# The second stage of an inverse transform, recorded with the last token group last, and a new issue order

## The chip, the cores and the metric

One Trainium2 chip, of which the kernel uses one core. The metric is the device time of one execution in microseconds. Matrix products run on TensorE (PE in the profile; its weight loads are PEld), element-wise work on VectorE (DVE) and ScalarE (ACT); transfers are issued mostly from SyncE's queue (SP) and are carried out by 16 DMA engines.

## The reference

The input `A_u` is 2048 tokens by 512 channels, all float32. It is normalised over the channels (xn). One branch is a state-space convolution along the tokens: a kernel K of 2048 taps per channel is built from 128 complex exponentials, and xn is convolved with it through transforms of twice the length. The other branch is a spatial-shift MLP. The output is gated and added to the input:

```
x = A_u
xn = layernorm(x)
K = einsum("dn,dnl,dn->dl", C, exp(dt*A*l), dt*B).real
s = irfft(rfft(pad(xn)) * rfft(pad(K)))[:L] + xn * Dskip
h = gelu(layernorm(xn) @ w1)                    # 512 -> 512
hs = concat(h shifted by +1, -1, +2, -2 tokens per channel quarter) @ w2
x1 = xn + hs
b = x1 + gelu(layernorm(x1) @ w3) @ w4          # 512 -> 1376 -> 512
out = x + s * silu(b)
```

## The kernel before

The tokens lie in the tile `X` as 128 partitions by 16 positions `s` by 512 channels. Two positions make a *group*; there are eight, and `GROUPS` is 1, 2, 3, 4, 5, 6, 7, 0, the order in which the MLP takes them. The convolution works on two halves of 256 channels, called a (`hf` 0) and b (`hf` 1) here.

The work is recorded in this order: loads; `params` (phases and magnitudes of the exponentials); `token_mixing` (first normalisation, w1, the shift and w2, the first transform stage of xn, preparation of w3 and w4 as pairs of float16); `tables(0)`, which builds K for half a in eight chunks (waves on ACT, products on DVE, sums on PE, stored to DRAM); the MLP of two groups; `kstage1(0)` and `products(0)` (transform of K, product of the spectra, first inverse stage for half a, result stored to `scr_Zda`); `tables(1)`; the MLP of the other six groups; `kstage1(1)` and `products(1)` (the same for half b, result to `scr_Zdb`); `gate` (a silu per group over the finished MLP result in `X`); `inverse` for both halves and all groups; `finish` per group (adds the input `xr`, stores to the output in four pieces of 128 KB).

`inverse(hf, g)` loads 0.5 MB of the intermediate result (`zin`), runs 16 small matrix products with `is2` into a pair of PSUM banks, and multiplies that half of the group's channels of `X` by the result. It takes its pair from `pp_pair`, which alternates between `duo[2]` and `duo[3]` (pc and pd in the profile, both 128 x 2 x 512). `products(1)` calls `pp_pair` 16 times ahead of it, so the first `inverse` gets pd. A later product into a pair has to wait until the multiplication that reads the earlier one is done. The multiplication of a group in turn has to follow the group's silu, and the silu the group's last down-projection (`mlp`, accumulated in `duo[0]`, pa in the profile; the up-projections go to pb).

Recording doesn't set the order in which things are issued. Every recorded operation (some are groups made with `plan.together`) goes through `Plan.add`, which finds what it depends on from the places that it reads and writes, in the recorded order. `Plan.order` then simulates the four queues (PE, ACT, DVE, SP) with estimated costs: at each step it takes the queue that is free first and, among its operations that are ready, the one with the smallest due time. The due times are the table `DUE`, one number per recorded operation. Constants correct them: `SWITCH` is added where ACT would have to load another function table, `KEEP` where PE would change the part of its array that it uses, `PREFERP`, `AVOIDP`, `PREFER`, `AVOID` where an operation may run on ACT or on DVE. So the result is a fixed list for each queue, which the engine works off in order. `ISSUE` is the estimated time that a transfer takes on its issuing queue, `TURNED` the estimated time of a transposing transfer on the DMA engines; the transposing transfers turn the normalised MLP input (`x1s`) into `x1T`.

## Time and profile before

| | us |
|---|---|
| median of 3 runs (lowest, highest) | 564.03 (563.72, 564.52) |
| the profiled execution | 563.24 |
| span of the profiled execution, first to last instruction | 561.4 |

The profile is of one execution; its span leaves out what lies before the first and after the last instruction. The mean granted TensorE clock of this execution was 0.991. All instructions that went through the planner carry line L532, where it issues them, so they are told apart by their tiles: x1T, w3h, ghl, w4h, pa and pb belong to the MLP, pt, mag and pab to the tables, kin, uin, pr to the products of spectra, zin to `inverse`, xr to `finish`. L529 is the loading of a function table on ACT. The DMA transfers over the whole span:

| | MB |
|---|---|
| read from HBM | 64.46 |
| written to HBM | 37.75 |

### The profile page before, as it was taken

Reading aid. Unit: us, or ns where it says so; the run is one execution under the profiler, and the core shown is the slowest. Engines: PE = TensorE matmul, PEld = TensorE weight load, DVE = VectorE, ACT = ScalarE, POOL = GpSimd, SP = SyncE. Lnnn points to the kernel's source line nnn. Section 1 sums busy time; section 2 is a strip of 40 time slices with the busy share of each in tenths; the row PEclk is TensorE's granted clock in tenths of the full one; section 3 lists DMA queues with packets and bytes.
Section 4 is the critical chain, followed back from the end, with each engine's and each line's share of the span. In section 5 each row is a group of like instructions: output and inputs, shape, how many; then the busy total and the mean of one; then the engine's idle time right before and its main releaser. Section 6 shows DMA issues by size and latency. Waiting matters only on the chain.

```text
span 561.4 us, 14315 instructions
## 1 busy us (share of the span) xinstructions
PE 530.3 (94%) x6098; PEld 348.1 (62%) x6098; DVE 452.7 (81%) x748; ACT 395.1 (70%) x573; POOL 0.7 (0%) x6
## 2 busy tenths in 40 slices
PE   9879999999999979999999999999999999999982
PEld 9866776767435438556577567557656567566530
DVE  5799996599999999999999999998344357753466
ACT  3789997699983989998899997976326424232520
POOL 0000000000000000000000000000000000000000
PEclk9999999999999999999999999999999999999996
DMA  8952767762666442576532745346898959949987
GB/s 212 234 163 66 242 219 257 238 201 76 214 209 218 147 97 79 103 225 226 144 105 62 176 141 133 86 161 190 242 291 288 303 173 284 263 165 255 280 261 219
DMA packets 86593, 107.35 MB, mean 191 GB/s; under 512 B 31680, under 2 KB 65728, under 8 KB 85632
## 3 DMA queue, kind: packets, MB, share of 16 engines
q1 hardware_dynamic: 85760, 104.33, 63.0%
q10 hardware_dynamic: 768, 2.10, 1.2%
q8 instruction: 48, 0.79, 0.6%
q14 instruction: 17, 0.14, 0.1%
HBM read 64.46 MB, written 37.75 MB: 182 GB/s over the span
## 4 chain that ended last, share of the span: by engine, by line
PE 65%; DVE 14%; DMA 8%; ACT 8%; issue 1%; SPq 1%; DVEq 0%; ACTq 0%
PE pb L532 26%; PE pa L532 21%; PE pc L532 10%; PE pd L532 8%; DVE pt L532 6%; DMA X<-in_A_u_dram 4%; DVE X L532 3%; ACT pt L532 3%; ACT mag L532 2%; DVE stats L532 2%; DMA wst<-in_B_w_dram 1%; DMA x1T<-x1s 1%; SPq L532 1%; ACT L529 1%; DMA scr_Kfa<-k1e 1%
## 5 line engine op out<-in xcount | busy, mean ns | idle before, releaser
L532 PE MATMUL pb<-x1T,w3h 128*128 128x256 f16 (+1 forms) x1056 | 123.0, 273 | 0.9 <-DMA x1T<-x1s 0.9
L532 PE MATMUL pa<-w4h,ghl 128*128 128x512 f16 (+1 forms) x528 | 120.9, 379 | 0.0
L532 PEld LDWEIGHTS <-w3h 128*128 128x128 f16 (+1 forms) x1056 | 102.4, 100 | 25.6 <-issue 11.3
L532 PEld LDWEIGHTS <-ghl 128*128 128x128 f16 (+1 forms) x528 | 49.6, 98 | 62.2 <-issue 7.1
L529 ACT ACT_TABLE_LOAD x54 | 69.3, 1283 | 5.2 <-DMA out_dram<-X 3.6
L532 ACT ACTIVATE pt<-pt 128x2048 f32<-128x2048 int32 x32 | 60.8, 1904 | 1.9 <-DVE pt L532 1.7
L532 PE MATMUL pb<-xT,w 128*128 128x256 f32 x256 | 59.6, 383 | 1.1 <-ACT xT L532 1.1
L532 DVE SCALAR_TENSOR_TENSOR ghl<-g,wsc,ghl 128x512 f16<-128x512 f32 (+1 forms) x48 | 33.5, 699 | 32.4 <-ACT ghl L532 32.3
L532 DVE TENSOR_TENSOR pt<-mag,pt 128x1024 f32<-128x1024 f32 x48 | 57.5, 1214 | 0.1
L532 PE MATMUL pd<-w,hT 128*128 128x512 f32 x116 | 52.9, 599 | 3.2 <-DVE X L532 2.3
L532 PEld LDWEIGHTS pb<-xT,w 128*128 128x128 f32 x256 | 47.1, 190 | 13.1 <-issue 3.2
L532 ACT ACTIVATE g<-pb,wsc 128x512 f32<-128x512 f32 (+1 forms) x48 | 30.9, 650 | 33.6 <-PE pb L532 31.2
L532 ACT ACTIVATE mag<-par 128x128 f32<-128x128 f32 x160 | 41.2, 454 | 4.6 <-DMA X<-in_A_u_dram 3.8
L532 ACT ACTIVATE ghl<-g,wsc 128x512 f16<-128x512 f32 (+1 forms) x33 | 22.4, 681 | 24.5 <-PE pa L532 23.5
L532 PEld LDWEIGHTS pd<-w,hT 128*128 128x128 f32 x116 | 21.4, 190 | 29.0 <-issue 23.9
L532 DVE TENSOR_TENSOR pt<-pt 128x2048 f32<-128x2048 f32 x16 | 36.5, 2282 | 2.0 <-ACT pt L532 2.0
L532 PEld LDWEIGHTS pc<-pt 128*32 128x32 f32 x2048 | 29.8, 110 | 10.5 <-issue 6.7
L532 PE MATMUL pc<-pt 128*32 128x64 f32 x2048 | 34.0, 220 | 2.1 <-DVE pt L532 1.8
L532 ACT ACTIVATE pt<-pt,halfpi 128x2048 f32<-128x2048 f32 x16 | 31.9, 1999 | 0.1
L532 DVE TENSOR_TENSOR pr<-pd,uin 128x1024 f32<-128x1024 f32 x16 | 19.1, 1217 | 11.7 <-PE pd L532 11.7
L532 DVE TENSOR_TENSOR pt<-pab 128x1024 int32<-128x1024 f32 x16 | 19.4, 1215 | 10.1 <-PE pc L532 10.1
L532 DVE TENSOR_TENSOR pr<-pd,kh 128x1024 f32<-128x1024 f32 x16 | 19.2, 1217 | 2.9 <-PE pd L532 2.9
(155 smaller groups left out, 753.8 us busy)
## 6 DMA issues: line engine op xcount, KB each, us to landing
wst<-in_B_w_dram SPq DMA_DIRECT2D x20, 512.0 KB, 3.8
scr_Ud<-ue SPq DMA_DIRECT2D x16, 512.0 KB, 4.0
uin<-scr_Ud SPq DMA_DIRECT2D x32, 256.0 KB, 4.5
cst<-c_gp SPq DMA_DIRECT2D x16, 384.0 KB, 4.6
scr_Uh<-uh SPq DMA_DIRECT2D x8, 512.0 KB, 5.2
scr_Kfa<-k1e SPq DMA_DIRECT2D x8, 512.0 KB, 2.8
kin<-scr_Kfa SPq DMA_DIRECT2D x16, 256.0 KB, 3.5
scr_Zda<-z1e SPq DMA_DIRECT2D x8, 512.0 KB, 5.6
```

Source lines behind the costliest of these rows:

```text
L529: self.engines["ACT"].preload_act_table_set(SETS[table])
L532: ins = [getattr(self.engines[op.eng], name)(*args, **kw).ins for name, args, kw in op.calls]
```

## The change

Three things change. In the recording, `inverse` runs over both halves for the first seven of `GROUPS`, and only then over both halves for the last one, group 0. For group 0 both halves write into one pair, always `duo[2]`, half a into the first 256 columns of each bank and half b into the other 256, and one multiplication over all 512 channels follows the second half; the first half returns without one. The number of matrix products is the same, there is one DVE operation less (1751 recorded operations, not 1752).

In the planner's estimates a transposing transfer takes 1.25 on its issuing queue, not 0.45, and 1.55, not 1.4, on the DMA engines.

And the whole table of due times is another, with another set of the constants that go with it. The diff without the table:

```diff
-TURNED = 1.4
+TURNED, TURN_ISSUE = 1.55, 1.25
 ISSUE = 0.45
-SHIFT, KEEP = 0.09, -134.72
+SHIFT, KEEP = 0.09, -41.4
...
-SWITCH = 57.29
-PREFERP, AVOIDP = 156.76, -96.02
-PREFER, AVOID = 81.81, -92.31
+SWITCH = 196.28
+PREFERP, AVOIDP = 150.95, -129.56
+PREFER, AVOID = -68.73, 92.63
...
-                cost = ISSUE
-                dma = TURNED if name == "dma_start_transpose" else dma_cost(aps)
+                cost, dma = (TURN_ISSUE, TURNED) if name == "dma_start_transpose" else (ISSUE, dma_cost(aps))
...
-        py = pp_pair()[:, :, :DH]
+        pair = duo[2] if g == GROUPS[-1] else pp_pair()
+        py = pair[:, :, ch if g == GROUPS[-1] else slice(0, DH)]
         with plan.together(cost=0.46):
             for r in range(4):
                 for a in range(2):
                     h = slice(64 * a, 64 * a + 64)
                     T.matmul(py[32 * r : 32 * r + 32, a], is2[h], zin[h, ORDER[r]], start=True, stop=True)
+        if g == GROUPS[-1]:
+            if hf == 0:
+                return
+            ch, py = slice(0, D), pair
         Xh = X[:, 2 * g : 2 * g + 2, ch]
         V.tensor_mul(Xh, Xh, py)
...
-    for hf in range(2):
-        for g in GROUPS:
-            inverse(hf, g)
+    for some in (GROUPS[:-1], GROUPS[-1:]):
+        for hf in range(2):
+            for g in some:
+                inverse(hf, g)
```

The due times run from -3272 to 2643 before and from -7486 to 7590 after. Those of the spectrum products (`spectrum` and the first inverse stage on PE) of half b in recorded order, and of group 0's MLP on PE:

| | before | after |
|---|---|---|
| spectrum products of half b | 819 to 1258 | 5268 to 6378 |
| the last three units of them | 837 to 1197 | 5272 to 6378 |
| up- and down-projections of group 0 | 984 to 1882 | 4670 to 7590 |
| products of `inverse`, groups 1 to 7, half a | 663 to 2390 | 6277 to 7404 |
| products of `inverse`, groups 1 to 7, half b | 420 to 1576 | 5508 to 7421 |
| products of `inverse`, group 0, half a and b | 525 and 1326 | 6467 and 4686 |

294 rows, old and new, of the table DUE are left out of this document.

## The prediction

> **What bounds the kernel now.** I read the page first (engine shares and the span in slices), then the busy time by stages, then the timeline and the chain of waits at the end, then the transfers there. The page says which engine is nearly full:
>
> ```profile
> span 561.4 us, 14315 instructions
> PE 530.3 (94%) x6098; PEld 348.1 (62%) x6098; DVE 452.7 (81%) x748; ACT 395.1 (70%) x573; POOL 0.7 (0%) x6
> ```
>
> A share of 94% is a mean over stages, so I cut the span where its character changes (busy us of each engine per stage):
>
> ```profile
> 41.00:120.00 79.00, 77.89 (x637) 57.58 (x637) 67.17 (x145) 69.69 (x88) 0.00 (x0) 1.00 0.59 197
> 120.00:220.00 100.00, 92.23 (x1230) 51.92 (x1229) 99.81 (x153) 87.52 (x150) 0.00 (x0) 1.00 0.49 158
> 220.00:500.00 280.00, 278.21 (x3445) 180.13 (x3443) 222.68 (x322) 195.12 (x248) 0.00 (x0) 1.00 0.65 190
> 500.00:542.50 42.50, 42.50 (x397) 24.05 (x397) 19.07 (x26) 15.35 (x19) 0.00 (x0) 1.00 0.93 254
> 542.50:561.40 18.90, 5.52 (x129) 1.61 (x128) 13.31 (x15) 1.06 (x1) 0.00 (x0) 0.74 0.64 188
> ```
>
> The columns are length, then PE, PEld, DVE, ACT, POOL, the granted clock, the share of the DMA engines, GB/s. From 120 to 220 DVE is full (99.81 of 100) and PE waits for it (100 - 92.23 = 7.77 us idle). From 220 to 542.5 PE is full: 278.21 of 280, then 42.50 of 42.50. In the last 18.90 us PE has 5.52 us of work and DVE 13.31. So 18.9 us of the span are a tail in which the engine that bounds the rest is mostly free. The timeline shows what it is made of:
>
> ```profile
> 537.18 5.36 PE L532 MATMUL pa<-w4h,ghl 128*128 128x512 f16 x24
> ...
> 542.57 1.28 DVE L532 SCALAR_TENSOR_TENSOR X<-pa,wsc,X 128x1024 f32<-128x1024 f32 x1 [2.60 <-PE pa L532]
> ...
> 543.89 1.06 ACT L532 ACTIVATE X<-X 128x1024 f32<-128x1024 f32 x1 [1.78 <-DVE X L532]
> ...
> 545.10 0.67 PE L532 MATMUL pc<-zin,is 64*32 64x256 f32 x16
> ...
> 546.70 0.68 DVE L532 TENSOR_TENSOR X<-X,pc 128x512 f32<-128x512 f32 x1
> ...
> 547.43 0.67 PE L532 MATMUL pc<-zin,is 64*32 64x256 f32 x16 [1.66 <-DVE X L532]
> ...
> 549.16 0.67 PE L532 MATMUL pc<-zin,is 64*32 64x256 f32 x16 [1.06 <-DVE X L532]
> ...
> 551.02 0.75 PE L532 MATMUL pc<-zin,is 64*32 64x256 f32 x16 [1.19 <-DVE X L532]
> ...
> 552.88 1.11 PE L532 MATMUL pc<-zin,is 64*32 64x256 f32 x16 [1.10 <-DVE X L532]
> ...
> 554.81 1.23 DVE L532 TENSOR_TENSOR X<-X,xr 128x1024 f32<-128x1024 f32 x1
> ```
>
> The last down-projection of the MLP (group 0) ends at 537.18 + 5.36 = 542.54. Its result goes through DVE (1.28) and the silu of group 0 on ACT (1.06, ending 544.95). After that come products of `inverse`, each followed by a multiplication and an addition on DVE, one after the other, to 554.81 + 1.23 = 556.04; the rest to 561.4, 5.36 us, is the last output stores.
>
> Why are so many inverse products left for the end? `inverse` takes its PSUM pair from `pp_pair`, which alternates: recorded in the order a1 to a7, a0, b1 to b7, b0 (a, b the channel halves), pc serves a2, a4, a6, a0, b2, b4, b6, b0 in that order. The multiplication that empties pc after a0 needs the silu of group 0, which needs the end of the MLP. So b2, b4, b6 cannot start before about 545 however early their data are there; they are the products at 547.43, 549.16 and 551.02, each waiting for a DVE X. The recorded order alone holds them back.
>
> **The change, part by part.**
>
> *The recorded order.* Group 0 goes last in both halves. The pc pair now serves a2, a4, a6, b1, b3, b5, b7 and then group 0; pd serves the others. No product of groups 1 to 7 is behind group 0's silu any more. Eight products fall after 542.4 in the timeline (starts 542.46, 542.92, 544.50, 545.10 and the four above); six of them are of groups 1 to 7 and may now run beside the last MLP group. Their price there is PE time, since PE is full:
>
> ```profile
> 536.65 0.59 PE pd L532 x16
> 537.25 5.30 PE pa L532 x24
> ```
>
> In the chain a product put between down-projections took 0.59 us. Six cost 6 x 0.59 = 3.5 us; if both products of group 0 are put ahead too, 8 x 0.59 = 4.7. I take the middle, 4.1: the MLP ends at 542.55 + 4.1 = 546.65.
>
> *The work of DVE that goes with them.* Of the 13.31 us in the last stage only the accumulation (1.28), two multiplications (2 x 0.68) and one addition (1.23) belong to group 0; 13.31 - 1.28 - 1.36 - 1.23 = 9.4 us move ahead of the MLP's end. From 500 to 542.5 DVE was busy for 19.07 of 42.50 us, so there are 23.4 us of room: cost nothing. If that room were not there when it is needed (the data late), the 9.4 us would stay on the path; that is the second rival.
>
> *One product for group 0.* Two multiplications of 128x512 (0.68 each) become one of 128x1024. The nearest row of that size, with one operand in PSUM:
>
> ```profile
> L532 DVE TENSOR_TENSOR pr<-pd,uin 128x1024 f32<-128x1024 f32 x16 | 19.1, 1217 | 11.7 <-PE pd L532 11.7
> ```
>
> So 1.22 instead of 1.36, 0.14 us less on the path. PE does the same 2 x 16 matmuls; only their place in PSUM differs.
>
> *The new tail.* After the MLP's end: accumulation and the step to ACT, 543.89 - 542.55 = 1.34; silu 1.06; multiplication 1.22 with a gap of 0.05; addition 1.23 with 0.02; together 4.92. Then the stores, 5.36 as now. Sum 546.65 + 4.92 + 5.36 = 556.9, against 561.4: 4.5 us less. The profiled execution took 563.24 us with a span of 561.4 (1.84 around it), the median of the runs shown is 564.03. On its own time: 563.24 - 4.5 = 558.7. The 5.36 is an upper value: stores of eight groups are crowded there now, and later only group 0's four are left at the end:
>
> ```profile
> L532 SPq DMA_DIRECT2D out_dram<-X x16: 314/315/1632, 537.9 to 556.7; - x16
> L532 ACTq DMA_DIRECT2D out_dram<-X x16: 321/382/1577, 537.9 to 556.9; - x16
> ...
> DMA to landing us min/median/max: 1.9/3.4/5.2
> ```
>
> With two issues of 0.38 on one queue and the shortest landing, 1.9, it would be 2.7; that lowers the sum by at most 2.7. I keep 5.36, the row of this place.
>
> *Is there room on the DMA engines?* All groups' stores but the last must get out before the end. The transfers from 535 on (busy share in 40 slices of 0.66 us, GB/s):
>
> ```profile
> DMA  9999999999832490008985989898839887997000
> GB/s 349 348 348 348 348 349 352 371 408 349 317 143 93 112 279 6 0 0 199 199 304 168 217 174 304 267 323 298 304 81 292 317 286 273 217 323 267 19 0 0
> ```
>
> The first ten slices are loads of `zin`, at about 349 GB/s until some 541; then there is a hole, and then the stores. 32 stores of 128 KB are 4.19 MB, of which four (0.52) went before 542. The other 3.67 MB at 290 GB/s, a middle value of the store slices, take 12.7 us: from 541.1 to 553.8, ahead of the 556.9. At 217, a low slice, 16.9 us and with 1.9 of landing 559.9. So the DMA engines stand just behind the new path; this gives the upper end of the case, 559.9 + 1.84 = 561.7.
>
> *The planner's constants.* `TURNED` and `TURN_ISSUE` only change what the planner assumes of a transposing transfer, from 0.45 us on SP to 1.25. The trace has
>
> ```profile
> L532 SPq DMA_TRANSPOSE x1T<-x1s x16: 1238/1276/5401, 203.8 to 485.7; - x16
> ```
>
> a median of 1.276, so the plan was wrong by 0.8 us at 16 places and is right now. No instruction gets dearer or cheaper. What it hid was small; the page puts down 0.9 us of PE's idle time in the whole span to an x1T:
>
> ```profile
> L532 PE MATMUL pb<-x1T,w3h 128*128 128x256 f16 (+1 forms) x1056 | 123.0, 273 | 0.9 <-DMA x1T<-x1s 0.9
> ```
>
> *The new order everywhere else.* Every due time is replaced (and `SWITCH`, `KEEP`, the preferences), so all four queues may differ from the first load on. The same instructions are issued, so the PE total stays. What can change is PE's idle time between 41 and 500: 1.11 + 7.77 + 1.79 = 10.7 us from the table of stages. Nothing in the trace says where the new order stands; I cost it at nothing and bound it by half of that idle time either way, 5.3 us, since the other half would need DVE to have gaps to close, and from 120 to 220 it has 0.19 us.
>
> *A rule against the change.* PE's clock falls in the tail: 0.74 granted in the last stage, and the product at 552.88 took 1.11 where others took 0.67. The Trainium skill, "TensorE: Matmul & The Clock Gate", Part 1, says that the array runs at half its clock after a window of about 3.4 us without enough activity. The trace agrees. If group 0's products were left until PE had rested, they would cost 1.11 - 0.67 = 0.44 us more each, and the sum would be 559.1 with one of them on the path. PE is busy right up to the silu here, so I do not add it.
>
> **The rivals.**
>
> 1. *More than the tail.* The new order also closes half of PE's idle time between 41 and 500: 558.7 - 5.3 = 553.4. For it: 7.77 us of idle lie in one stage. Against: DVE is full there, so only another choice of its work, not more of it, could help.
>
> 2. *The change does not do what it says.* The PSUM pair is free, but the data of half b come late. Its loads:
>
> ```profile
> L532 SPq DMA_DIRECT2D zin<-scr_Zdb x8: 382/1386/3235, 522.3 to 533.5; - x8
> ...
> DMA to landing us min/median/max: 5.1/9.9/12.2
> ```
>
> The last is issued at 533.5 and lands near 541, as the full DMA slices show. If the second half's spectrum is not finished earlier against the MLP than now, and the products wait, the 9.4 us of DVE stay behind the MLP, and only 0.14 goes: 563.1. Against: between 541 and the new end of the MLP, 546.65, there are 5 us even then, and the due times of the last spectrum products stand to those of group 0's MLP much as before (the last three units 5272 to 6378 beside 4670 to 7590 now, 837 to 1197 beside 984 to 1882 then), so nothing in the diff puts the data later.
>
> 3. *The order in the stage that DVE bounds gets worse* (slower). From 120 to 220 PE lives on what DVE hands it, and after 220 PE is full, so idle time gained there is never made up. The unit by which an order can go wrong is a table chunk:
>
> ```profile
> L532 DVE TENSOR_TENSOR pt<-mag,pt 128x1024 f32<-128x1024 f32 x48 | 57.5, 1214 | 0.1
> ...
> L532 DVE TENSOR_TENSOR pt<-pt 128x2048 f32<-128x2048 f32 x16 | 36.5, 2282 | 2.0 <-ACT pt L532 2.0
> ...
> L532 DVE TENSOR_TENSOR pt<-pab 128x1024 int32<-128x1024 f32 x16 | 19.4, 1215 | 10.1 <-PE pc L532 10.1
> ```
>
> (57.5 + 36.5 + 19.4) / 16 = 7.1 us of DVE per chunk. One chunk done ahead of what PE needs gives 558.7 + 7.1 = 565.8. It decides against the change when PE's idle time between 41 and 500 passes 10.7 + 4.5 = 15.2 us.
>
> 4. *The products stand in front of the MLP and wait* (slower). PE takes its queue in order:
>
> ```profile
> 492.95 1.47 PE L532 MATMUL pb<-x1T,w3h 128*128 128x256 f16 x12 [0.87 <-DMA x1T<-x1s]
> ...
> 494.35 2.00 PE L532 MATMUL pc<-pr,cst 64*128 64x256 f32 x16
> ```
>
> Where it waited 0.87 us for an x1T ahead of 492.95, the product behind it started only after that. Eight `zin` tiles of 0.52 MB at 349 GB/s need 12.0 us; if all eight products were queued ahead of the last down-projections, PE would go at the pace of the loads and idle for 12.0 - 8 x 0.59 = 7.3 us: 558.7 + 7.3 = 566.0. The Trainium skill, the same page, Part 3 ("The mechanism"), says that matmuls start and end in program order; by that rule a product that waits for its load holds back every down-projection behind it. The trace agrees at 492.95. Against the rival: with two PSUM pairs at most two products can be ahead of their multiplications, so a queue of eight cannot form unless it is put there on purpose.
>
> **How the numbers follow.** Forecast 558.7, chance 0.50, its own range 556.0 (shorter stores) to 561.7 (DMA bound). Rival 1, 553.4: 0.17. Rival 2, 563.1: 0.15. Rival 3, 565.8: 0.11. Rival 4, 566.0: 0.07. The range reaches from 553.2, just under rival 1, to 564.5, over rival 2 and up to a part of a chunk; what lies outside is rivals 3 and 4 and a little of 1, 2 in 10. A measurement of this kernel can tell about 0.2% (1.1 us) from no change, so faster means under 562.9 and slower over 565.2: 0.67 (forecast and rival 1), 0.15 (rival 2), 0.18 (rivals 3 and 4).
>
> **What would show it.** Right: in the new timeline, from the end of the last pa matmul to the end of the span some 10.3 us instead of 18.9; at most two products after it; one multiplication 128x1024 of X by pc; the MLP's end at 546 to 547 and PE's idle time between 41 and 500 near 10.7. Rival 1 shows as the MLP's end well before 546; rival 2 as a row of X<-X,pc and X<-X,pd after it; rival 3 as an MLP's end past 551 with the idle time between 120 and 220; rival 4 as PE idle time put down to zin just ahead of the end. The forecast is wrong if the stores, not DVE, end last with full DMA slices.

## The result, and the profile after

| | before | after |
|---|---|---|
| median (lowest, highest), same chip | 564.27 (563.72, 564.76), 4 runs | 549.58 (548.68, 550.85), 4 runs |
| ratio, 95% interval | | 0.9741 [0.9718, 0.9765] |
| profiled execution / its span | 563.24 / 561.4 | 550.05 / 548.3 |

The change takes 14.7 us off. The forecast was 558.7, 4.5 us off, with a range that ended at 553.2: the sign was right, the size was missed by a factor of three, and the time lies below the range. The two profiled executions, from which the rows below are, stand 13.2 us apart.

In after, line L542 issues what L532 issued before, and L539 loads function tables. L541 (L531 before) issues *fillers*: products without use that the planner writes into PE's queue where it expects PE to wait. The stages of after, with the columns of the prediction's table (length; busy time of PE, PEld, DVE, ACT, POOL; granted clock; DMA share; GB/s):

```profile
41.00:120.00 79.00, 79.00 (x645) 58.91 (x643) 73.18 (x155) 72.80 (x87) 0.00 (x0) 1.00 0.65 216
120.00:220.00 100.00, 98.48 (x1283) 55.15 (x1283) 98.66 (x160) 94.95 (x169) 0.00 (x0) 1.00 0.54 156
220.00:500.00 280.00, 273.85 (x3431) 176.32 (x3428) 213.83 (x296) 191.66 (x242) 0.00 (x0) 1.00 0.62 191
500.00:529.50 29.50, 29.50 (x326) 18.26 (x326) 11.54 (x17) 11.47 (x14) 0.00 (x0) 1.00 1.00 288
529.50:548.30 18.80, 8.88 (x123) 3.73 (x120) 13.90 (x16) 2.85 (x3) 0.00 (x0) 0.81 0.75 221
```

Between 41 and 120 us DVE does 73.18 us of work where it did 67.17; between 120 and 220 ACT does 94.95 where it did 87.52, and PE waits 1.52 us where it waited 7.77. PE waits more than before from 220 to 500: 6.15 against 1.79. So time was gained ahead of 220 us, and in this execution a part of it was handed back later. How much differs from execution to execution: s1 and t1, two experiments below that keep after's order on PE there, wait 4.12 and 3.56 us from 220 to 500.

The end of after, in the timeline (start, length, engine, operation):

```profile
530.91 5.36 PE L542 MATMUL pa<-w4h,ghl 128*128 128x512 f16 x24
...
536.19 0.66 PE L542 MATMUL pc<-zin,is 64*32 64x256 f32 x16
536.30 1.28 DVE L542 SCALAR_TENSOR_TENSOR X<-pa,wsc,X 128x1024 f32<-128x1024 f32 x1
...
536.65 0.64 PE L542 MATMUL pd<-zin,is 64*32 64x256 f32 x16
...
537.82 1.28 ACT L539 ACT_TABLE_LOAD   x1 [7.26 <-DMA out_dram<-X]
...
538.23 1.10 PE L542 MATMUL pc<-zin,is 64*32 64x256 f32 x32 [0.95 <-DVE X L542]
538.70 2.35 DVE L542 TENSOR_TENSOR X<-X,xr 128x1024 f32<-128x1024 f32 x2
539.12 1.06 ACT L542 ACTIVATE X<-X 128x1024 f32<-128x1024 f32 x1
...
540.97 1.21 DVE L542 TENSOR_TENSOR X<-X,pc 128x1024 f32<-128x1024 f32 x1
542.21 1.22 DVE L542 TENSOR_TENSOR X<-X,xr 128x1024 f32<-128x1024 f32 x1
```

The MLP ends at 536.27 (542.54 before), the span 12.0 us later (18.9 before). Four products of 16 matmuls stand behind the MLP's end (the last row is group 0's two in one), where there were eight. Four more ahead of it cost some 2.4 us by the 0.59 of the prediction. So what the MLP's end waits for, that apart, was done 6.3 + 2.4 = 8.7 us earlier, and that is the part that the forecast did not have.

PE ends the MLP, so PE's own balance up to there says where these 8.7 us were. First all of PE's work, then the fillers alone (length; busy time of PE and PEld; the last three columns as above), in before and in after:

```profile
0.00:542.54 542.54, 524.82 (x5978) 346.50 (x5986) 439.36 (x733) 394.00 (x572) 0.70 (x6) 1.00 0.65 191
0.00:542.54 542.54, 22.42 (x192) 21.99 (x192) 1.00 0.65 191
```

```profile
0.00:536.27 536.27, 522.07 (x6002) 345.03 (x6010) 436.02 (x723) 399.18 (x585) 0.70 (x6) 0.99 0.65 195
0.00:536.27 536.27, 19.50 (x152) 18.95 (x152) 0.99 0.65 195
```

PE's idle time falls from 17.72 to 14.20 us and its fillers from 22.42 to 19.50: 3.5 and 2.9 us. The other work is as long (502.40 and 502.57 us) though four products more are in it; that is the rest, 2.2 us or so. Most of the fillers lie ahead of 41 us, and so does a part of the lead: the first w1 product starts at 38.88 us in after and at 40.81 in before.

The largest single difference shows on DVE. The timeline of before and that of after around 100 us:

```profile
104.16 1.23 DVE L532 TENSOR_TENSOR pt<-pab 128x1024 int32<-128x1024 f32 x1 [10.12 <-PE pc L532]
```

```profile
99.39 1.22 DVE L542 TENSOR_TENSOR pt<-par,ev 128x1024 int32<-128x1024 f32 x1 [3.63 <-PE pc L542]
```

DVE waits there for PE: the sums of the first table chunk go into the pair pc behind the last product of xn's first transform stage. In before that wait is 10.12 us long and the table work goes on at 104.16; in after it is 3.63 and the work goes on at 99.39.

The next landmark is the transform of K for half a (`kstage1(0)`, pc<-ksl,kk and pd<-ksl,kk): its first and last product in before, then in after.

```profile
230.95 0.70 PE L532 MATMUL pc<-ksl,kk 32*128 32x512 f32 x2
...
256.69 0.59 PE L532 MATMUL pd<-ksl,kk 32*128 32x512 f32 x2
```

```profile
223.33 0.70 PE L542 MATMUL pc<-ksl,kk 32*128 32x512 f32 x2
...
245.61 0.59 PE L542 MATMUL pd<-ksl,kk 32*128 32x512 f32 x2
```

So the lead is 4.8 us at DVE's restart, 7.6 at the first of these products and 11.1 at the last. The busy time up to that last product, before and then after:

```profile
0.00:257.20 257.20, 241.27 (x2410) 165.34 (x2410) 234.80 (x491) 220.11 (x352) 0.70 (x6) 1.00 0.59 178
```

```profile
0.00:246.10 246.10, 236.25 (x2352) 160.50 (x2352) 229.73 (x458) 221.50 (x352) 0.70 (x6) 0.99 0.63 185
```

Of the 11.1 us, DVE's idle time is 6.0 (257.20 - 234.80 = 22.40 against 16.37), and 5.1 is work that DVE no longer does ahead of this point (234.80 against 229.73): it goes to ACT or is done later. Of the 6.0 us of idle time, 1.4 lie ahead of 41 us and 6.0 between 41 and 120; behind that DVE waits 1.4 us more than before.

### The profile page after: what moved, and what is told of

The parts are those of the page before. It is cut to its first block, busy times and chain, and to the rows that moved or that the text cites. A ratio compares the mean times of both kernels' runs of the same rounds, so it can differ in the third digit from the quotient of the medians.

```text
span 548.3 us, 14226 instructions
## 1 busy us (share of the span) xinstructions
PE 524.2 (96%) x6058; PEld 345.9 (63%) x6058; DVE 443.2 (81%) x730; ACT 401.5 (73%) x587; POOL 0.7 (0%) x6
## 4 chain that ended last, share of the span: by engine, by line
PE 71%; DVE 11%; DMA 8%; ACT 6%; issue 2%; SPq 1%; DVEq 0%; ACTq 0%
PE pb L542 29%; PE pa L542 18%; PE pd L542 13%; PE pc L542 10%; DVE X L542 3%; DVE pt L542 3%; DMA cst<-c_gp 2%; ACT mag L542 2%; DMA zin<-scr_Zdb 1%; DMA X<-in_A_u_dram 1%; SPq L542 1%; DMA rawA<-in_A_A_re_dram 1%; ACT pt L542 1%; DVE ghl L542 1%; ACT L539 1%
## 5 line engine op out<-in xcount | busy, mean ns | idle before, releaser
L542 PE MATMUL pb<-x1T,w3h 128*128 128x256 f16 (+1 forms) x1056 | 122.9, 273 | 0.4 <-DMA x1T<-x1s 0.4
L542 PE MATMUL pa<-w4h,ghl 128*128 128x512 f16 (+1 forms) x528 | 122.3, 380 | 0.2 <-DVE ghl L542 0.2
L542 PEld LDWEIGHTS <-w3h 128*128 128x128 f16 (+1 forms) x1056 | 102.8, 100 | 26.7 <-issue 10.8
L542 PEld LDWEIGHTS <-ghl 128*128 128x128 f16 (+1 forms) x528 | 49.3, 98 | 61.8 <-issue 8.7
L542 ACT ACTIVATE pt<-pt 128x2048 f32<-128x2048 int32 x32 | 60.7, 1906 | 2.0 <-DVE pt L542 1.9
L542 PE MATMUL pb<-xT,w 128*128 128x256 f32 x256 | 59.1, 383 | 1.1 <-ACT xT L542 1.1
L542 DVE TENSOR_TENSOR pt<-mag,pt 128x1024 f32<-128x1024 f32 x48 | 57.5, 1217 | 1.2 <-ACT pt L542 1.1
L542 DVE SCALAR_TENSOR_TENSOR ghl<-g,wsc,ghl 128x512 f16<-128x512 f32 (+1 forms) x48 | 33.4, 701 | 30.9 <-ACT ghl L542 30.6
L542 PE MATMUL pd<-w,hT 128*128 128x512 f32 x116 | 53.1, 599 | 1.4 <-DVE X L542 1.4
L542 PEld LDWEIGHTS pb<-xT,w 128*128 128x128 f32 x256 | 47.2, 190 | 10.7 <-issue 2.7
L542 ACT ACTIVATE g<-pb,wsc 128x512 f32<-128x512 f32 (+1 forms) x48 | 30.5, 649 | 27.3 <-PE pb L542 26.3
L542 ACT ACTIVATE ghl<-g,wsc 128x512 f16<-128x512 f32 (+1 forms) x38 | 26.0, 689 | 28.1 <-PE pa L542 28.0
L542 ACT ACTIVATE mag<-par 128x128 f32<-128x128 f32 x160 | 41.0, 454 | 2.8 <-DMA is<-c_is 2.6
L542 PEld LDWEIGHTS pd<-w,hT 128*128 128x128 f32 x116 | 21.3, 190 | 27.4 <-issue 24.2
L542 DVE TENSOR_TENSOR pt<-pt 128x2048 f32<-128x2048 f32 x16 | 36.4, 2283 | 0.2 <-ACT pt L542 0.2
L542 DVE TENSOR_TENSOR pr<-pd,uin 128x1024 f32<-128x1024 f32 x16 | 19.3, 1221 | 20.3 <-PE pd L542 20.3
L542 PEld LDWEIGHTS pc<-pt 128*32 128x32 f32 x2048 | 29.7, 110 | 9.2 <-issue 8.7
L542 PE MATMUL pc<-pt 128*32 128x64 f32 x2048 | 33.0, 220 | 0.7 <-issue 0.7
L542 ACT ACTIVATE pt<-pt,halfpi 128x2048 f32<-128x2048 f32 x16 | 32.0, 2000 | 0.2
L542 ACT COPY z1e<-pc 128x1024 f32<-128x1024 f32 x7 | 7.1, 1013 | 22.6 <-PE pc L542 22.6
L542 DVE TENSOR_TENSOR pt<-par,ev 128x1024 int32<-128x1024 f32 x16 | 19.5, 1216 | 4.2 <-PE pc L542 4.2
```

The lines of the kernel that those rows point to most:

```text
L542: ins = [getattr(self.engines[op.eng], name)(*args, **kw).ins for name, args, kw in op.calls]
```

## The experiments

Each kernel was timed beside before on the same chip. "us" is (ratio - 1) x 564.2, so that kernels that were timed beside different runs of before can be compared; the intervals are 0.8 to 1.7 us to either side, and a difference between two rows is uncertain by some 1.5 to 2 us. After stands at -14.6 on this scale.

| run | median | ratio to before [95%] | us |
|---|---|---|---|
| e1_record_only | 566.46 | 1.0029 [1.0011, 1.0048] | +1.6 |
| e2_record_tail | 560.83 | 0.9939 [0.9920, 0.9958] | -3.4 |
| e3_order_tail | 551.16 | 0.9776 [0.9747, 0.9806] | -12.6 |
| e4_order_to_280 | 549.78 | 0.9744 [0.9722, 0.9767] | -14.4 |
| p1_dve_gap_before | 573.18 | 1.0155 [1.0138, 1.0172] | +8.7 |
| p2_dve_gap_after | 558.76 | 0.9905 [0.9891, 0.9920] | -5.4 |
| p3_pe_before | 569.69 | 1.0108 [1.0091, 1.0125] | +6.1 |
| p4_pe_after | 551.13 | 0.9782 [0.9752, 0.9812] | -12.3 |
| h1_order_to_100 | 556.82 | 0.9868 [0.9845, 0.9890] | -7.4 |
| h2_order_to_196 | 557.00 | 0.9866 [0.9839, 0.9892] | -7.6 |
| h3_order_to_256 | 550.16 | 0.9749 [0.9725, 0.9774] | -14.2 |
| t1_tail | 550.67 | 0.9757 [0.9735, 0.9779] | -13.7 |
| k1_later_transform | 551.38 | 0.9785 [0.9766, 0.9805] | -12.1 |
| p5_dve165_before | 570.28 | 1.0116 [1.0095, 1.0136] | +6.5 |
| p6_dve165_after | 557.19 | 0.9884 [0.9854, 0.9914] | -6.5 |
| p7_pe300_after | 552.10 | 0.9799 [0.9774, 0.9824] | -11.3 |
| s1_sums_earlier | 548.89 | 0.9743 [0.9722, 0.9765] | -14.5 |

### The two halves of the change, each alone

**e1**, before with the new recording, group 0's pair and single product included, and nothing else (the due times stay with their operations):

```diff
...
-    for hf in range(2):
-        for g in GROUPS:
-            inverse(hf, g)
+    for some in (GROUPS[:-1], GROUPS[-1:]):
+        for hf in range(2):
+            for g in some:
+                inverse(hf, g)
```

> The recording of after alone (group 0 last, one product into one pair), with the due times and constants of before carried over operation by operation; the one product of group 0 takes the due time of half b's. Theory A (the gain of 14.7 us has two parts: 4 to 5 us from the recorded order at the end, as forecast, and some 10 us from the other order of the work ahead of 280 us): the recording changes only what can be issued near the end, and due times that were found for another end leave part of it unused: 560 to 565 us, all of the gain in front missing. Theory B (all of the gain comes from the recorded order at the end, the pair that group 0 no longer blocks): close to after, 549 to 553 us. The trace tells: PE idle between 41 and 500 us stays at 10.7 us by A, and the first up-projection of the last six groups stays at 211.8 us.

Theory A, a little past the upper end of its range: no gain, 1.6 us lost. The MLP ends where it did, and the tail is 21.0 us long. Its last rows in the timeline:

```profile
554.69 1.96 PE L530 MATMUL pc<-zin,is 64*32 64x256 f32 x32 [0.84 <-DVE X L530]
...
556.82 1.22 DVE L530 TENSOR_TENSOR X<-X,pc 128x1024 f32<-128x1024 f32 x1 [0.93 <-PE pc L530]
```

The pair is free of group 0, but the old due times put its product last of all. The recording only permits; the due times have to make use of it.

**e2**, e1 with other due times from the gates on (the last lines of the table):

```diff
-    -1210.66, 524.87, -1177.14, 1326.23, 1263.25, -1094.13, -597.53, -1059.1, -1159.34, 1253.29, -2000.61, -609.67,
+    -763.23, -1736.71, -1397.81, -590.47, -1414.5, -2397.48, -970.85, -3484.74, 739.29, -1409.68, -903.34, 22.42,
```

> The recording of after and, for everything ahead of the gates, the due times of before; the due times of the last operations (gates, second stages, finishing) are searched anew for this recording. So it is the end of the change on the front of before. Theory A: the MLP's end at about 542.5 us plus up to 4 us for products moved ahead of it, and 10 to 12 us behind it in place of 18.9: 557 to 561 us, 3 to 7 us of the 14.7. Theory B (the whole gain is the recorded order): 549 to 552 us. Theory C (nothing from the recording; the whole gain from the order in front): 562.5 to 565 us.

Theory A. The MLP's last products in its timeline:

```profile
543.02 4.06 PE L530 MATMUL pa<-w4h,ghl 128*128 128x512 f16 x18
```

So the MLP's end is 547.08, where the forecast had 546.65, and the span of 559.7 ends 12.6 us later, where it had 10.3. (This execution took 562.56 us, 1.7 more than the median.) On the front of before the change's end is worth 3.4 us (the interval gives 2.4 to 4.5).

**e3**, the counterpart: after with the old recording, and other due times from the gates on.

```diff
...
-    for some in (GROUPS[:-1], GROUPS[-1:]):
-        for hf in range(2):
-            for g in some:
-                inverse(hf, g)
+    for hf in range(2):
+        for g in GROUPS:
+            inverse(hf, g)
```

> The opposite half: the recording of before (half a of all groups, then half b; group 0 in two products), the due times and constants of after for everything ahead of the gates, and for the last operations due times searched anew for this recording. So it is the front of after with the end of before. Theory A: the front's gain of some 10 us stays and the 4 to 5 us of the recorded order are missing: 553 to 556 us, the first up-projection of the last six groups near 190.7 us as in after. Theory B: 562 to 565 us, no gain left without the recording. Theory C: 549 to 551 us, as after.

Between A and C: 12.6 us of the gain are there without the new recording. Its MLP ends early, and its tail is as long as in before:

```profile
524.41 5.36 PE L539 MATMUL pa<-w4h,ghl 128*128 128x512 f16 x24
```

That is 529.77, 12.8 us ahead of before's 542.54, and 18.3 us from there to the end of its span, 548.1. Against after the missing recording costs 2.0 us by the ratios, with intervals that overlap.

**e4**, a list in place of the planner's loop; the entries up to 280 us of after's plan, then those of e2:

```diff
-        ops = self.ops
...
+        out = []
+        for word in SEQUENCE.split():
...
+            out.append(op)
+        return out
```

> The recording of after, and the issue order of after for all that its plan starts ahead of 280 us; all the rest in the order of e2 (before's order in the middle, with the end searched for the recording). Written out as a fixed list. Theory A with its place (the gain in front is made ahead of 280 us: 130 more up-projection and reduction products done by 212 us): it keeps nearly everything, 550 to 554 us, and the MLP ends at 536 to 541 us. Theory D (the gain is made behind 280 us, by fewer waits of PE there): 557 to 561 us, as e2.

Theory A with its place: 549.78, nothing of the gain is missing. What the change does behind 280 us and ahead of the gates is worth nothing that can be measured. From e2 to e4, which differ ahead of 280 us only, it is 11.0 us.

### What a microsecond is worth, and where

**p1** and **p2**, more work in front of the DVE operation that ends the long wait (p2: the same with 693 in after):

```diff
+            if op.idx == 694:
+                op.calls = [("tensor_reduce", self.probe, dict(axis=AX.XY, op=ALU.max))] * 8 + list(op.calls)
```

> Before, with eight additional reductions (128x1024, some 1.14 us apart, 9.1 us together) on DVE, put ahead of the multiplication that starts at 104.16 us, so into the 10.12 us in which DVE waits there. Every theory: within 1 us of before (563.5 to 565.5), since nothing else is in that wait. If it costs more, the wait is not idle time that could have been used.

> The same eight reductions in after, ahead of the multiplication at 99.39 us, where DVE waits only 3.63 us: the tables' work behind it starts some 5.5 us late, about when it started in before. Theory A1 (the front gained because DVE begins the tables earlier and is the engine that sets the pace up to 212 us): 4 to 5.5 us over after, 553.5 to 555.5. Theory A2 (in the new order PE sets the pace, and DVE's head start is only slack): 549.5 to 551.5.

Both missed, since the reductions did not fall into the wait. They are part of the operation that waits, and so they came behind it, in p1 and in p2:

```profile
105.14 10.00 DVE L558 TENSOR_REDUCE warm<-ident 128x1 f32<-128x1024 f32 x8 [10.15 <-PE pc L558]
```

```profile
99.25 10.00 DVE L568 TENSOR_REDUCE warm<-ident 128x1 f32<-128x1024 f32 x8 [3.68 <-PE pc L568]
```

So the reductions became another experiment: DVE's table work 10.0 us later, in both kernels. That costs 8.7 us in before and 9.2 in after (from -14.6 to -5.4). From about 100 us on, 1 us on DVE costs 0.9 us of the kernel, in the old order and in the new one alike. That is A1's mechanism at about its own price (4 to 5.5 us for 5.5); the slack of A2 is not there.

**p3** and **p4**, more work on PE at some 131 us (p4: the same with 428 in after):

```diff
+            if op.idx == 427:
+                name, args, kw = op.calls[0]
+                op.calls = [(name, args, dict(kw, start=True, stop=True))] * 6 + list(op.calls)
```

> Before, with six additional products of the w2 kind (128x512 float32, 0.92 us each by the 3.70 us of four, 5.6 us together) on PE at 132.5 us, in the stage where DVE is busy 99.8 of 100 us and PE waits 7.8 us and issues 1.7 us of fillers. A1 (DVE sets the pace there in before): 564 to 566 us, at most 2 us more, the waits of PE in that stage shrinking by what is added. A2 (PE sets the pace in before, too): 568.5 to 570 us.

> The same six products in after at 131.0 us, where PE waits 1.5 us between 120 and 220 us and issues no fillers. If the new order has moved the bound of this stage to PE (A2, or PE and DVE alike): 4 to 5.6 us over after, 553.5 to 555.5. If DVE still sets the pace alone (A1): 549.5 to 551.5.

Neither theory has both: 6.1 us in before, as A2 says, and 2.3 in after, as A1 says. The block on PE grew in both from 3.70 to 8.85, so by 5.15; in p4:

```profile
130.16 8.85 PE L569 MATMUL pd<-w,hT 128*128 128x512 f32 x20
```

Table sums and w2 results that DVE waits for are issued on PE behind these products, so a delay on PE is passed on. In p3 DVE's busy time from 120 to 220 us falls from 99.81 to 94.94:

```profile
120.00:220.00 100.00, 94.94 (x1089) 50.90 (x1088) 94.94 (x144) 83.01 (x143) 0.00 (x0) 0.98 0.49 154
```

In p4 it falls as much (98.66 in after), and yet the end moves by less:

```profile
120.00:220.00 100.00, 98.48 (x1257) 53.36 (x1256) 93.71 (x149) 89.74 (x164) 0.00 (x0) 1.00 0.47 145
```

Why is not shown. A guess would be that waits of PE behind 220 us take up the delay, but p4 still has 3.38 us of them from 220 to 500, about as many as s1 and t1 (4.12 and 3.56), which have no such delay. And the 2.3 is uncertain by some 2 us.

**p5** and **p6**, five reductions in the stretch that the prediction called full:

```diff
+            if op.idx == 769:
+                op.calls = [("tensor_reduce", self.probe, dict(axis=AX.XY, op=ALU.max))] * 5 + list(op.calls)
```

> Before, with five more reductions on DVE (6.2 us together, by the 10.00 us that eight took) at about 165 us, in the stretch from 120 to 220 us where DVE is busy 99.81 of 100 us. If a full DVE is the bound of that stretch, as the prediction took it: 5 to 6.2 us more, 569 to 570.5. If it is full only because work has piled up that may as well be done later: 564.3 to 566.

> The same five reductions in after at about 169.7 us, where DVE is busy 98.66 of 100 us and PE 98.48. DVE still the bound of the stretch: 554.5 to 556. PE the bound and DVE's work movable: 549.5 to 551.5.

DVE is the bound of that stretch in both: 6.5 and 8.1 us for some 6.2 (p6, with 557.19, is even past the range of that theory). The stretch in p5 and in p6:

```profile
120.00:220.00 100.00, 86.63 (x1054) 46.40 (x1053) 98.84 (x147) 80.82 (x134) 0.00 (x0) 0.97 0.48 152
```

```profile
120.00:220.00 100.00, 92.66 (x1220) 50.01 (x1221) 96.06 (x142) 86.60 (x153) 0.00 (x0) 0.95 0.45 142
```

PE pays: 5.6 us less busy time than in before, 5.8 less than in after, and a granted clock of 0.97 and 0.95 where it was 1.00.

**p7**, PE further back, in the stretch where PE is nearly full:

```diff
+            if op.idx == 1269:
+                name, args, kw = op.calls[0]
+                op.calls = [(name, args, dict(kw, start=True, stop=True))] * 46 + list(op.calls)
```

> After, with 46 more products of the up-projection's kind on PE at about 297 us (0.112 us each by the 5.41 us of 48 rows, 5.1 us together). Theory P (PE's throughput sets the end from there): 2 to 5 us more, 551.5 to 554.7, less than 5.1 only by what the waits of 3.3 us for cst near 450 us take up. Theory S (the chain through tables and transforms sets it, PE has slack): 549.5 to 551.

Theory P, in the lower part of its range: 2.5 us by the medians, 3.3 by the ratios, for 5.1. PE's idle time from 220 to 500 us is 2.54 us in p7 and 6.15 in after. The list of PE's waits (us in total, times, longest) has for cst, the largest in after, these rows in after, p7, t1 and s1:

```profile
PE pd L542 <- DMA cst<-c_gp: 3.3, 2, 2.0
```

```profile
PE pd L569 <- DMA cst<-c_gp: 0.2, 1, 0.2
```

```profile
PE pd L568 <- DMA cst<-c_gp: 1.0, 3, 0.5
```

```profile
PE pd L566 <- DMA cst<-c_gp: 0.8, 2, 0.6
```

t1 and s1 have after's order on PE in this stretch and no delay, and yet they wait for cst only 1.0 and 0.8 us. So most of after's 3.3 belongs to that one execution. Against t1 and s1, p7 waits 1.0 and 1.6 us less from 220 to 500; that is what the traces show taken up of the 5.1, and the rest of the difference is within the uncertainty.

### Where in the front

**h1**, **h2**, **h3** are e4 with the cut at 100, 196 and 256 us of the plan. These plan times run some 5 to 8 us ahead of the trace. The list at the cut of h1, entries as operation and engine, against that of after:

```diff
 695D 296P 712D 696A
-297P 709D 688D 718D
+297P 298A 710D 688A
```

> As e4, but the order of after only for what its plan starts ahead of 100 us, the rest in the order of e2. With it DVE's chain of table work restarts at 99.4 us and not at 104.2. Theory S (the gain in front is the table chain running earlier, in steps: 4.8 us at that restart, 7.6 us at the first product of the transform of K, 11.0 us at its last): by the price measured when the restart was delayed (9.1 and 9.2 us for 10.0), 4.8 us make 4.4: 556.4 against e2's 560.8, between 555 and 558. Theory W (the gain hangs on the whole order and is lost at any seam): 560 to 562.

> The same with the order of after up to 196 us of its plan, all that lies ahead of the transform of K for half a. Theory S: 6 to 7.6 us of the chain are there, 553 to 555.5. Theory W: 558 to 562.

> The same up to 256 us, the transform of K for half a included, where before issues 25.2 us from the first product of it to its last and after 21.8 us, with fewer MLP products between its four groups. Theory S: all of the 11 us are there but for the seam, 550 to 552. Theory W: 555 to 560.

h1 agrees with theory S: 4.0 us less than e2. DVE's restart stands at 98.38 us in its trace and at 104.75 in e2's, so the gain is 0.6 us per us of it, less than the 0.9 of p1 and p2. h3 agrees too: everything is there. h2, with 557.00, lies between the two theories and is no better than h1. Its chain of waits has one long entry, at this row:

```profile
219.51 4.85 PE L565 MATMUL pb<-x1T,w3h 128*128 128x256 f16 x22 [6.03 <-ACT g L565]
```

At the seam ACT takes the MLP's gelu behind table work, and PE stands still for 6.03 us. That is a loss at the seam, as theory W says, and it hides what the order from 100 to 196 would give. So the gain has two steps that can be told apart: 4.0 us ahead of 100, and 6.8 us (h1 to h3) from 100 to 256. DVE's balance up to the last product of the transform, in h1 and in h3:

```profile
0.00:251.80 251.80, 237.87 (x2384) 163.25 (x2384) 237.40 (x493) 219.40 (x349) 0.70 (x6) 0.99 0.60 181
```

```profile
0.00:244.00 244.00, 233.90 (x2352) 158.23 (x2352) 229.28 (x458) 221.06 (x351) 0.70 (x6) 1.00 0.62 185
```

Step one fills DVE's waits: idle 14.4 us in h1, 22.4 in before, with 2.6 us more work done. Of these 8.0 us, 2.1 lie ahead of 41 us, where h1 has after's order too, and 5.9 between 41 and 120; which of the two carries the 4.0 us was not tried. Step two takes work away: DVE is as idle in h3 (14.7), but has 8.1 us less to do up to this point (237.40 against 229.28). The largest part is this group of h1, two copies of the transform's results, which h3 does on ACT:

```profile
L565 DVE COPY k1e<-pc 128x1024 f32<-128x1024 f32 x2 | 2.4, 1218 | 0.0
```

The others are pieces of the MLP's input, of its weights and of the next table, done later.

**k1** undoes the part of step two in which the transform of K ends earlier, on PE, in after's list:

```diff
-929P 872P 865P 934P 893P 878P 894P 879P
+929P 872P 865P 893P 878P 894P 879P 934P
```

> After, with one thing moved: the up-projections that PE issues behind the fourth group of the transform of K for half a (5.41 us at 246.13 us) are issued ahead of that group, so that the transform ends some 5.4 us later and PE issues the same work in all. Theory S (what counts is how early the chain table, transform of K, products, next table runs): 4 to 5.4 us over after, 553.5 to 555. Theory P (from 212 us on PE's throughput alone sets the end, and there the order of its work is free): 549.3 to 551.

Between the theories: 1.8 us over after by the medians, 2.5 by the ratios. The transform's last product is 6.9 us later than in after, and half b's first only 2.8. In after these two are at 245.61 (above) and 413.81. The rows of k1, with the moved products ahead of them:

```profile
245.73 5.40 PE L566 MATMUL pb<-x1T,w3h 128*128 128x256 f16 x48 [1.73 <-ACT g L566]
...
252.46 0.59 PE L566 MATMUL pd<-ksl,kk 32*128 32x512 f32 x2
...
254.15 1.99 PE L566 MATMUL pc<-pt 128*32 128x64 f32 x128 [1.10 <-ACT k1e L566]
...
416.59 0.70 PE L566 MATMUL pc<-ksl,kk 32*128 32x512 f32 x2
```

The move itself makes PE wait, 1.73 us for the gelu ahead of the moved products and 1.10 us for a copy behind the transform, waits that after does not have there. Together, 2.83 us, they are as much as k1 costs. So by the ratios a transform that ends 6.9 us later costs 2.5 us at most, about a third of step two. That the rest is the work which DVE doesn't do in that time is argued from the balance; it was not undone alone.

### Two tries at more

**s1** issues the first chunk's sums ahead of a part of the w1 products in front of them:

```diff
-293P 294P 668P 667P
+293P 668P 667P 294P
```

> After with one change of order on PE at 95 us: the first table chunk's sums (1.99 us at 97.33 us) are issued ahead of the second half of the w1 products that stand in front of them (3.72 us at 93.68 us, so 1.86 us), since their pair is free from 94.81 us on. DVE's wait of 3.63 us for these sums should shrink to some 1.8 us. Theory D (DVE sets the pace of the stretch up to 212 us, at the 0.9 us per us that the delay by 10.0 us showed): 1.6 us less than after, 547.7 to 548.3. Theory E (the w1 products that are now later hold up something that is as tight, the next transposition and through it PE or ACT): 549.3 to 552.

The median, 548.89, lies between the two ranges. DVE goes on 1.8 us earlier and then waits again, for the second chunk's sums; the two rows:

```profile
97.61 1.23 DVE L566 TENSOR_TENSOR pt<-par,ev 128x1024 int32<-128x1024 f32 x1 [2.00 <-PE pc L566]
...
103.72 1.23 DVE L566 TENSOR_TENSOR pt<-par,ev 128x1024 int32<-128x1024 f32 x1 [1.48 <-PE pc L566]
```

The wait is in two pieces now and as long in all (3.5 against 3.63), and the transform of K begins at 223.23 where it began at 223.33. The median is 0.7 us lower than after's, the ratio the same: no gain can be told. So the gain of theory D is missing, as theory E says; but what DVE waits for in its place is the second chunk's sums, not the transposition that theory E named.

**t1**, another end for after:

```diff
+            eng = self.pool if op.idx == 1732 else self.engines[op.eng]
...
+            if op.idx == 1515:
+                table = self.ops[1647].table
+                self.engines["ACT"].preload_act_table_set(SETS[table])
```

> After with another end: ACT loads the silu's function table behind its last other activation (about 531 us) and not between the last stores and the silu; the last but one addition of the input (128x1024, 1.22 us) runs on GpSimd and not on DVE; group 0's multiplication follows the silu with one addition ahead of it and not two. Theory T1 (behind the MLP's end DVE is the bound: it is busy without a gap from 536.30 to 543.43 us, and the table load lies beside it): one addition less on DVE, 1.1 us less, 548.4 to 548.7 if 549.6 is after's. Theory T2 (GpSimd's addition takes more than 3 us or slows DVE's beside it, so that its store ends last): 549.6 to 551.

Theory T2, by its second clause: 550.67, no gain. The addition on GpSimd and the one on DVE beside it:

```profile
536.04 2.35 POOL L568 TENSOR_TENSOR X<-X,xr 128x1024 f32<-128x1024 f32 x1 [534.73 <-DMA out_dram<-X]
536.53 2.94 DVE L568 TENSOR_TENSOR X<-X,xr 128x1024 f32<-128x1024 f32 x1
```

DVE's addition took 2.94 us and not 1.22. What DVE saved by the one addition it lost in the other; from the MLP's end (533.99) to the last addition's end (541.86) are 7.87 us, and in after 7.16. From there to the end of the span are another 6.94 us, in after 4.87: from 538 to 540 us, where the two additions end, hardly anything is stored (4 and 0 GB/s), and the stores end later.

## Why the prediction was right and wrong

**The recorded order and the MLP's end at 546.65.** The time agrees, 547.08 in e2, but by luck. Four products moved and not six to eight, so four are left behind the MLP in e2 and in after, where at most two were foreseen; by the forecast's own 0.59 us that is 2.4 and an end at 544.9. The other 2.1 us came from elsewhere: the same 192 fillers take 24.04 us in this trace and 22.42 in before's, and the execution is a long one. And the recorded order alone does not hold the products back, as the prediction says: with it changed and nothing else (e1) nine products of 16 matmuls stand behind the MLP's end, where there were eight.

**One product for group 0.** As forecast: 1.21 us for 1.22, one row of 128x1024.

**DVE's 9.4 us into its room ahead of the MLP's end.** Partly. Behind the MLP's end after has 1.28 + 0.68 + 0.68 + 2.35 + 1.21 + 1.22 = 7.4 us of DVE's work, not the 3.9 of group 0 alone, so 5.9 of the 13.31 moved. The room was there, but with two products of other groups left their two multiplications and two additions were left too.

**The new tail of 10.3 us.** Too short: 12.0 us in after, 12.6 in e2. The sum had 4.92 us from the MLP's end to the last addition's end; the timeline has 7.16 (536.27 to 543.43). The terms that it lacked are the two multiplications and two additions of other groups that DVE does ahead of group 0's multiplication (0.68 + 0.68 + 2.35 us), and the function table that ACT loads ahead of the silu, 1.28 us. The stores are 4.87 us, for 5.36. That the table load decides is not shown: DVE is busy without a gap beside it, and t1, which took it out of the way, changed DVE's work too.

**The sum of 4.5 us for the recorded order.** e2 gives 3.4 with 4.5 at the edge of its interval, so the size was about right, with a tail that was 2.3 us too short and an MLP's end that fits by luck. It needs the due times, too: with the recording alone (e1) it is a loss of 1.6. On the front of after it is worth 2.0 (e3 against after), uncertain by some 2 us, so whether the two terms simply add can't be told. The two terms as measured, 3.4 (e2) and 11.0 (e2 to e4), make the whole 14.4 of e4; the forecast had 4.5 and nothing.

**DMA engines and planner's constants.** That the stores are not the bound was not shown. The forecast named full DMA slices at the end as a sign against it, and after's are mostly full; the busy tenths in 40 slices from 535 us to the end of its span:

```profile
DMA  9995999799998979768999999888997898200000
```

The engines are busy for half to nearly all of each slice until some 546.6 us, and the last stores are issued by 543.9. DVE's last addition starts them, but an earlier one would still find the engines busy. The planner's constants act only through the order and the fillers that they make the planner write; they were not tried by themselves.

**"The new order everywhere else", costed at nothing, at most half of PE's idle time, 5.3 us.** This is the step that failed. It was worth 11.0 us (e2 to e4). Two things were wrong in it. The bound was taken from PE's idle time between 41 and 500 us, 10.7 us, and that is only a part of the time in which PE waits. Up to the MLP's end before has 17.72 us of idle time and 22.42 of fillers, which the rows count as busy. From e2 to e4, whose MLP ends at 547.08 and 535.41, idle time falls by 5.4 us and fillers by 4.2, and the same products take 2.1 less. And PE's waiting does not say what could shorten it: DVE sets the pace ahead of some 220 us, as p1, p2, p5 and p6 show with 0.9 to 1.3 us for each us (in before PE does so too at 131 us, by p3: 6.1 for 5.15). The second thing is the reason given, that DVE would need gaps and has 0.19 us of them from 120 to 220: it looked at one stage only. The row above it in the same table says 67.17 of 79.00, 11.8 us of gaps, and one of them is 10.12 us long, in a row that the prediction quoted for another purpose (the 10.1 behind pt<-pab). Work that is done in the gap is work that need not be done in the full stage behind it. h1 has 3.63 us of that gap left and gains 4.0 us.

**Rival 1, 553.4.** Its sign to look for came true, the MLP's end well before 546. Its mechanism, less idle time on PE, is there for a part: from 41 to 500 us it falls from 10.7 to 7.7 in after's trace (0 + 1.52 + 6.15), to 5.7 in s1 and 5.1 in t1, so by 3 to 5.6 us where the rival had 5.3. The rest of the gain is not in it. The sentence against it, that only another choice of DVE's work could help, names what goes with the second step: 8.1 us of work taken from DVE's stretch (h1 to h3, 6.8 us).

**Rival 3.** Its premise, DVE as the bound from 120 to 220 us, holds (p5). It was used for a loss only; the same premise says that an order which spares DVE there gains.

**Rivals 2 and 4** did not occur: no wait of PE for zin stands in the chain of waits. The sign of rival 2, X<-X,pc and X<-X,pd of other groups behind the MLP's end, is there for two multiplications (at 537.50 and 538.10), but the last loads of half b were issued by 521.9 and landed within 9.6 us, so the data were there and the order put these products last.

**What stays open.** How the 6.8 us of step two divide between 100 and 196 us and the rest, since the seam of h2 covers it; whether the work taken from DVE is what k1 does not explain; how much of step one was won ahead of 41 us; why a delay of PE costs 6.1 us in before and 2.3 in after; and how much of the end the stores set.

## What to carry to other kernels

When a list of work is ordered anew, look at the engine that is full in one stage and count its idle time over all stages ahead of that: a full stage is shortened by work that was done in an earlier gap, or need not be done yet. One probe of some us on each engine at each stage tells which engine sets the pace; a busy share of 99% does not (in after PE's and DVE's were both over 98% from 120 to 220 us, and a us cost 0.4 on one and 1.3 on the other). And products that only fill a wait belong to the waiting, not to the work. A freed buffer gives nothing by itself until the order is found that uses it.

## What the runs showed of the hardware

**An addition on GpSimd stops DVE.** In t1 GpSimd's addition ran from 536.04 to 538.39 and DVE's, started at 536.53, ended at 539.47, that is 1.08 us behind GpSimd's end, for a length of 1.22 alone: as if it had begun only then. The Trainium skill, "SBUF — State Buffer", "SBUF: two separate sides", says that DVE, with two inputs in SBUF, and GpSimd share a pair of ports that one instruction holds for its whole length while the other waits. These two rows agree.

**PE's waits can cost more than their length.** In p6, where DVE holds PE up, 16 products of w2 behind a wait of 6.64 us take 10.11 us; in after, behind 0.49 us, the same 16 take 7.13. The row of p6, that of after, and p6's slice of these 10.11 us (the granted clock is the third number from the end):

```profile
180.35 10.11 PE L568 MATMUL pd<-w,hT 128*128 128x512 f32 x16 [6.64 <-DVE X L568]
```

```profile
174.49 7.13 PE L542 MATMUL pd<-w,hT 128*128 128x512 f32 x16 [0.49 <-DVE X L542]
```

```profile
180.35:190.46 10.11, 10.11 (x20) 4.11 (x24) 8.08 (x8) 3.70 (x2) 0.00 (x0) 0.70 0.42 119
```

PE is full in that slice and gets a clock of 0.70; after's slice has 1.00. In p1, where PE is empty from 118 to 124 us, the clock is 0.67 there and 0.76 in the next 6 us, when PE is full again. So the wait is followed by 2.98 us of slower work. That goes the way of p6's 8.1 us for 6.2, but how much of that difference it makes is not shown: it lies within the interval.
